# Staggering the two score lanes of a clustered-attention kernel, moving its small pieces, and viewing three VectorE operands interleaved

## The chip, the cores and the metric

The kernel runs on one core of a Trainium2 chip. The metric is the device time of one execution in microseconds; three runs of the kernel before gave 782.86 to 784.72 us, with a median of 783.25 us. Names used for the engines: TensorE (PE in the profile, with PEld for its weight loads), VectorE (DVE), ScalarE (ACT), GpSimd (POOL), and SyncE (SP), which here only issues DMAs.

## The reference

There are 4 batches with 8 heads each, 768 positions and head width 64. Queries and keys are each assigned to one of 16 clusters, and a query attends only to keys of its own cluster. The result is put through a rotation by an angle that depends on the data, a mixing over the positions with two 768 x 768 weights, and a channel layer.

```
q_assign = argmax(q/|q| . centroid/|centroid|)         # per head, 16 clusters; k_assign likewise
mask     = q_assign[:, None] == k_assign[None, :]
scores   = where(mask, q @ k.T / sqrt(64), -1e9)
attn     = softmax(scores)                             # row maximum subtracted, exp, divided by the row sum
x        = (attn @ v) as (batch, 768, 512)
theta    = x @ w_theta;  zr, zi = x*cos(theta), x*sin(theta)
u        = x + w_tok_r @ zr + w_tok_i @ zi
out      = u + relu(u @ w_ch)
```

The weights w_theta, w_tok_r, w_tok_i and w_ch arrive as 64-bit floats; the kernel turns them into 32-bit ones by integer operations, and then into a high and a low part.

## The kernel before, in words

**Two stages.** The attention stage runs from the start to about 440 us, the mixing stage (rotation, mixing, channel layer) from there to the end. The change touches the attention stage alone; the mixing stage uses what it leaves.

**Pairs, lanes, units, bodies.** Two heads are handled together as a pair, so there are 16 pairs. The two heads of a pair are two lanes, `j` = 0 and 1: one has its 64 rows in partitions 0 to 63, the other in 64 to 127, so that a product of one lane and a product of the other can run on TensorE at the same time. A pair has 12 units: two halves of the queries (`a`, 384 columns each) by six blocks of 128 keys (`i`). The main loop at the end of the attention stage handles two units in one body, so a pair takes six bodies, and there are 96 bodies with scores.

**What a unit computes.** `score_products` lists four products for each lane that add up in one PSUM bank, a tile `sc`: high by high, high by low, low by high, and a mask product `mk` by `mq` that also carries the row maximum. `exps` (ScalarE) takes the exponential of the bank into a tile `at`. `add_exps` (GpSimd) adds tiles `at` in threes into `acc`. `weighted` multiplies `at` with the values into the bank `av`, in the following body. Row maxima are found ahead of use: `max_products` computes, ten units ahead (`LEAD`), an approximate score `m` over all 768 keys (two halves of two products for each lane, in a tile of two banks), and `max_of` (VectorE) reduces it. There are two such tiles, one for each lane, so the products of a body can be written only when the reduces of the body before have read theirs. PSUM has eight banks: four in the two `m` tiles, three in the pool that `bank` and the `sc` tiles share, and one for `av`.

**How the products are put in order.** `interleave` takes lists of products and issues them step by step, one of each list. Before, a body issues in this order: `both` (four steps, both lanes of unit u), `scores_beside_max` for j = 0 (four steps, lane 0 of unit u+1 beside the maximum products of lane 1), the weighted products of the two units before, and `scores_beside_max` for j = 1 (four steps). Each group of four steps is followed by its exponentials and its reduce.

**The small pieces.** All else is cut into small pieces and hung at a unit by `at_unit` and `stages`; `pieces` issues what is due at three places of a body. These are, with their tables: the assignment of the clusters for a pair two pairs ahead (`assign`, at `A_UNITS`: load, logits, their transposes and maximum, first maximum, transpose of the result, two rounds of DMA through DRAM, two ScalarE steps for `mq`, one VectorE step for `mk`); the high and low parts of q and k (`HI_UNITS` on ScalarE, `LO_UNITS` on GpSimd); conversion of one block of weights for each pair (`to_f32` and `split_w`, at `W_UNITS`: DMA, ScalarE, four VectorE steps, and then a copy on ScalarE and a subtraction on GpSimd); the row sums (`add_sums` on VectorE at `ADDS`, `sums` at `SUMS`), the division (`normalise` at `NORM`), and `shift_row`, which transposes the maxima and puts them into `mq`.

**What fixes the order.** After each body, `in_order` ties every instruction of an engine to the one before it, SyncE's DMAs too. So within the attention stage every engine works in the order in which the code issues, and an instruction that waits holds up all that its engine has behind it.

Of the kernel before, what the change touches and what calls it, by code (L numbers as in the profile page):

```python
# [2 lines left out]

# [6 lines left out]
F32 = mybir.dt.float32  # L10
# [20 lines left out]
ADDS = (8, 13)  # L31
EARLY = 3
NAT = 6
# [10 lines left out]
def kernel(  # L44
# [79 lines left out]
    def to_f32(src, cols, new):  # L124
# [16 lines left out]
        with behind(weights_after[0]):  # L141
            nc.scalar.activation(out=w, in_=high.bitcast(F32), func=AF.Abs)
        yield
        nc.vector.tensor_scalar(
            out=w, in0=w, scalar1=F64_LEAST, scalar2=F64_MOST, op0=ALU.max, op1=ALU.min)
        yield
        nc.vector.tensor_scalar(
            out=wi, in0=wi, scalar1=5, scalar2=2, op0=ALU.logical_shift_left, op1=ALU.logical_shift_right)
# [182 lines left out]
    def assign(pi):  # L331
# [15 lines left out]
        if "mt" in st.get(pi - 2, {}):  # L347
            mt = st[pi - 2].pop("mt")
            rt = mt[0:NG, P:2 * P]
            nc.tensor.transpose(out=rt, in_=rr, identity=identf)  # L350
# [11 lines left out]
        for n, x in enumerate("qk"):  # L362
# [11 lines left out]
            out=st[pi]["mk"], in0=cl["k"], scalar1=mcl, scalar2=mbi, op0=ALU.not_equal, op1=ALU.mult)  # L374
# [59 lines left out]
    def shift_row(pi, a):  # L434
# [5 lines left out]
        if a == 1 and 0 < pi < NPAIR - 2:  # L440

            s["mt"] = mt
        else:
            shift_out(pi, a, mt)
# [10 lines left out]
    def score_products(u, j, banks=None):  # L455
# [5 lines left out]
        sc = banks[:, j] if banks else ps.tile([P, 512], F32, tag="bank", name=f"sc{u}_{j}")  # L461
        sc = s["sc", j] = sc[:, 0:HS]
# [4 lines left out]
    def exps(u, j):  # L467

        pi, a, i = split_u(u)
        s = st[pi]  # L470
        last_exp[0] = nc.scalar.activation(out=s["at", a, i][:, j], in_=s["sc", j], func=AF.Exp, scale=SCALE)  # L471
# [291 lines left out]
    for pi in range(NPAIR):  # L763
        u = NU * pi
        if pi > 0:
            prepare(pi, g2 if pi == 2 else assign(pi))
            at_unit(u - NU + 7, load_v, pi)
# [15 lines left out]
    u = 0  # L783
    while u <= NUT or todo:
# [8 lines left out]
        if 0 <= u < NUT:  # L793
            both(score_products, u, exps)
            if u == 0:
                for j in range(2):
                    interleave(max_products(ahead - 2, j))
                    max_of(ahead - 2, j)
                for n, x in ((1, "mk"), (0, "mq")):
                    nc.scalar.activation(  # L800
                        out=st[1][x], in_=turn_one_hot(1, n), func=AF.Identity,
                        **(dict(scale=BIG, bias=mbi) if n else {}))
                nc.gpsimd.memset(cl["q"], -100.0)
            add_exps(u)
            if ahead < NUT:
                scores_beside_max(u + 1, ahead, 0)
        pieces(u - 0.5)
        if 0 < u <= NUT:
# [4 lines left out]
            if ahead >= NUT:  # L813
                weighted_out(u - 1)
        pieces(u)
        if 0 <= u < NUT:
            if ahead < NUT:
                scores_beside_max(u + 1, ahead, 1)
            else:

                both(score_products, u + 1, exps, *([m_tile(f"sc{u + 1}")] if u < NUT - 6 else []))
            add_exps(u + 1)
        if 0 < u and ahead < NUT:
            weighted_out(u - 1)
# [274 lines left out]
```

## Time and profile before

| | us |
|---|---|
| median of three runs | 783.25 |
| the profiled execution | 783.16 |
| its span, first to last instruction | 781.4 |
| TensorE busy, whole span | 773.2 (99%) |
| VectorE busy | 567.8 (73%) |
| ScalarE busy | 388.2 (50%) |
| GpSimd busy | 500.6 (64%) |
| one pair in the middle of the attention stage (201.58 to 227.54) | 25.96 |
| of it TensorE / VectorE / ScalarE / GpSimd busy | 25.96 / 24.61 / 17.58 / 25.40 |
| one of the first pairs (96.08 to 122.59) | 26.51 |

How to read it: the ends of matmuls are modelled and matmuls overlap, so that a busy TensorE may still issue more densely; the starts of its instructions tell more than its busy time. Busy time of VectorE and GpSimd contains time in which an instruction has started and stands still. The granted TensorE clock is 1.00 in all stretches.

### The profile page before, as it was taken

Reading aid. Unit: us, or ns where it says so; the run is one execution under the profiler, and the core shown is the slowest. Engines: PE = TensorE matmul, PEld = TensorE weight load, DVE = VectorE, ACT = ScalarE, POOL = GpSimd, SP = SyncE. Lnnn points to the kernel's source line nnn. Section 1 sums busy time; section 2 is a strip of 40 time slices with the busy share of each in tenths; the row PEclk is TensorE's granted clock in tenths of the full one; section 3 lists DMA queues with packets and bytes.
Section 4 is the critical chain, followed back from the end, with each engine's and each line's share of the span. In section 5 each row is a group of like instructions: output and inputs, shape, how many; then the busy total and the mean of one; then the engine's idle time right before and its main releaser. Section 6 shows DMA issues by size and latency. Waiting matters only on the chain.

```text
span 781.4 us, 14422 instructions
## 1 busy us (share of the span) xinstructions
PE 773.2 (99%) x5592; PEld 573.0 (73%) x5592; DVE 567.8 (73%) x689; ACT 388.2 (50%) x780; POOL 500.6 (64%) x289
## 2 busy tenths in 40 slices
PE   9999999999999999999999999999999999999998
PEld 6666565566666666566665588898889988899998
DVE  6789999999999999999989587844344444533322
ACT  3565757576767676767556455432333132503310
POOL 4568888989999999988987667561225112422231
PEclk9999999999999999999999999999999999999999
DMA  4113324432443244425354377124101411120001
GB/s 143 42 60 101 113 63 127 134 100 85 145 134 113 73 144 134 133 69 168 114 203 131 85 219 198 20 58 145 28 15 28 163 27 28 17 92 15 1 21 61
DMA packets 81708, 73.24 MB, mean 94 GB/s; under 512 B 59544, under 2 KB 65512, under 8 KB 81256
## 3 DMA queue, kind: packets, MB, share of 16 engines
q1 hardware_dynamic: 81634, 72.32, 31.2%
q8 instruction: 44, 0.72, 0.4%
q14 instruction: 24, 0.20, 0.1%
q10 hardware_dynamic: 6, 0.00, 0.0%
HBM read 56.89 MB, written 15.31 MB: 92 GB/s over the span
## 4 chain that ended last, share of the span: by engine, by line
PE 92%; DVE 4%; DMA 1%; issue 1%; SPq 1%; ACT 1%; POOL 0%; DVEq 0%
PE y L967 26%; PE sc L408 25%; PE av L543 15%; PE tp L643 7%; PE cy L990 5%; PE m L408 4%; PE cp L990 3%; PE lg L286 1%; PE sm L510 1%; PE y L990 1%; PE lt L299 1%; DVE acc L486 1%; DVE mk L373 1%; PE mt L438 1%; DVE nm L430 1%
## 5 line engine op out<-in xcount | busy, mean ns | idle before, releaser
L471 ACT ACTIVATE at<-sc 128x384 f32<-128x384 f32 x384 | 173.7, 495 | 97.6 <-PE m L408 57.5
L430 DVE TENSOR_REDUCE nm<-m 128x1 f32<-128x768 f32 x192 | 179.8, 946 | 21.0 <-PE m L408 19.9
L482 POOL TENSOR_TENSOR acc<-at,at 128x768 f32<-128x768 f32 x64 | 129.1, 2016 | 34.8 <-ACT at L471 34.8
L408 PE MATMUL m<-hk,hq 64*128 64x384 f32 x384 | 147.7, 385 | 0.8 <-DVE nm L430 0.6
L543 PE MATMUL av<-at,vt 128*64 128x384 f32 x768 | 145.3, 499 | 0.2 <-ACT xt L558 0.2
L918 POOL TENSOR_TENSOR zlc<-ab,zhc 128x512 fp32r<-128x512 f32 x24 | 32.9, 1371 | 162.7 <-ACT zhc L916 162.7
L482 POOL TENSOR_TENSOR acc<-acc,at 128x768 f32<-128x768 f32 x64 | 131.8, 2060 | 7.9 <-ACT at L471 5.7
L408 PE MATMUL m<-mk,mq 64*128 64x384 f32 x384 | 128.1, 334 | 0.0
L408 PE MATMUL sc<-hq,hk 64*128 64x384 f32 x384 | 117.7, 390 | 1.1 <-ACT at L471 0.9
L408 PEld LDWEIGHTS sc<-hq,hk 64*128 64x128 f32 x384 | 56.1, 183 | 61.8 <-issue 24.9
L408 PE MATMUL sc<-lq,hk 64*128 64x384 f32 x384 | 98.3, 335 | 0.0
L408 PE MATMUL sc<-mq,mk 64*128 64x384 f32 x384 | 97.8, 334 | 0.0
L408 PE MATMUL sc<-hq,lk 64*128 64x384 f32 x384 | 97.6, 333 | 0.0
L543 PEld LDWEIGHTS av<-at,vt 128*64 128x64 f32 x768 | 46.5, 136 | 58.6 <-issue 53.7
L408 PEld LDWEIGHTS m<-hk,hq 64*128 64x128 f32 x384 | 70.5, 183 | 3.3 <-DVE nm L430 2.6
L408 PEld LDWEIGHTS m<-mk,mq 64*128 64x128 f32 x384 | 71.1, 185 | 0.2 <-DVE mk L715 0.2
L649 DVE TENSOR_SCALAR kk<-tp 128x512 int32<-128x512 f32 x24 | 16.4, 685 | 73.2 <-PE tp L643 73.2
L486 DVE TENSOR_TENSOR acc<-acc,acc 128x768 f32<-128x768 f32 x30 | 69.0, 2302 | 0.0
L616 ACT CAST xh<-xT 128x512 fp32r<-128x512 f32 x23 | 14.3, 621 | 99.3 <-PE tp L643 99.3
L981 POOL TENSOR_TENSOR ul<-xT,uh 128x384 fp32r<-128x384 f32 (+1 forms) x36 | 33.5, 964 | 35.5 <-ACT uh L980 33.8
L408 PEld LDWEIGHTS sc<-mq,mk 64*128 64x128 f32 x384 | 55.3, 184 | 0.0
L408 PEld LDWEIGHTS sc<-hq,lk 64*128 64x128 f32 x384 | 55.2, 184 | 0.0
(174 smaller groups left out, 1716.3 us busy)
## 6 DMA issues: line engine op xcount, KB each, us to landing
vt<-in_v_dram SPq DMA_DIRECT2D x16, 384.0 KB
rb<-sd SPq DMA_DIRECT2D x32, 192.0 KB
xT_d<-xt SPq DMA_DIRECT2D x16, 384.0 KB
xb<-xT_d SPq DMA_DIRECT2D x96, 64.0 KB
rawq<-in_qT_dram SPq DMA_DIRECT2D x15, 384.0 KB
rawk<-in_kT_dram SPq DMA_DIRECT2D x15, 384.0 KB
w<-in_wrT_dram SPq DMA_DIRECT2D x6, 768.0 KB
xT<-xT_d SPq DMA_DIRECT2D x3, 1536.0 KB
```

Of the source, the lines that this page charges most:

```text
L408: nc.tensor.matmul(out, lhsT=stat[r, cols], rhs=mov[r, over], start=start, stop=stop)
L430: nc.vector.tensor_reduce(out=s["nm", a][:, j, i // 2:i // 2 + 1], in_=s["m", j][:, :, 0:HS], op=ALU.max, axis=AX.XY, negate=True)
L471: last_exp[0] = nc.scalar.activation(out=s["at", a, i][:, j], in_=s["sc", j], func=AF.Exp, scale=SCALE)
L482: last_acc[0] = nc.gpsimd.tensor_tensor(out=s["acc", a, x], in0=prev, in1=at, op=ALU.add)
L486: nc.vector.tensor_tensor(out=s["acc", a, 0], in0=s["acc", a, 0], in1=s["acc", a, 1], op=ALU.add)
L543: nc.tensor.matmul(s["av"][64 * j:64 * j + 64], lhsT=s["vt"][:, i, j, :], rhs=s["at", a, i][:, j], start=(i == 0), stop=(i == NT - 1))
L643: nc.tensor.matmul(tp, lhsT=xx[:, c, :], rhs=w_th[c][k], start=(n == 0), stop=(n == 3 * NCT - 1))
L649: nc.vector.tensor_scalar_mul(kk, tp, INV_2PI)
L918: nc.gpsimd.tensor_tensor(out=zl, in0=tr, in1=zh.bitcast(F32), op=ALU.subtract)
L967: last_mix[0] = nc.tensor.matmul(y_at(b, d, c0, c1), lhsT=zz[:, d * P:(d + 1) * P], rhs=ww[:, c0:c1], start=first and lead, stop=last, ski ...
L981: nc.gpsimd.tensor_tensor(out=ul[:, d, :], in0=x, in1=uh[:, d, :].bitcast(F32), op=ALU.subtract)
L990: nc.tensor.matmul(cp, lhsT=w_c[d][k][:, e * P:(e + 1) * P], rhs=uu[:, d, :], start=(n == 0), stop=(n == 3 * NCT - 1), skip_group_check=True)
```

## The change

1. **Order of the products.** The scores of unit u in lane 0 are begun at the end of the body before (three of four steps, kept in `begun`). A body first issues the pieces due and the weighted products of the two units before, and then one run of twelve steps. In each step a product of one list stands beside a product of another that is one or three steps behind it: the end of lane 0's scores beside the start of lane 1's; the maximum products of lane 0 beside the rest of lane 1's scores; and so on, up to the three first products of the next body's unit in lane 0. Exponentials and reduces follow each list's last step. The two reduces of a body so follow three steps behind each other, with no piece between them.
2. **Small pieces.** The pieces move to other units: `ADDS`, `A_UNITS`, `HI_UNITS`, `LO_UNITS`, `W_UNITS`, and the load of v. The transposes `lt` take a bank of the shared pool and no longer an `m` tile; the transposes `mt` and `rt` no longer share a bank, and the maxima are sent out at once.
3. **Views.** Three VectorE forms work on the same bytes through views in which the second half of the columns is interleaved with the first: the mask `mk`, and the clamp and the shift in `to_f32`.
4. **Buffers.** `at` has 5 buffers in place of 6. For the last units, which have no maximum products, each lane's scores get an `m` tile of their own.

```diff
-ADDS = (8, 13)
+ADDS = (6.5, 14)
-NAT = 6
+NAT = 5
...
+        wt, wit = (x.rearrange("p (a b) -> p b a", a=2) for x in (w, wi))
         nc.vector.tensor_scalar(
-            out=w, in0=w, scalar1=F64_LEAST, scalar2=F64_MOST, op0=ALU.max, op1=ALU.min)
+            out=wt, in0=wt, scalar1=F64_LEAST, scalar2=F64_MOST, op0=ALU.max, op1=ALU.min)
         yield
         nc.vector.tensor_scalar(
-            out=wi, in0=wi, scalar1=5, scalar2=2, op0=ALU.logical_shift_left, op1=ALU.logical_shift_right)
+            out=wit, in0=wit, scalar1=5, scalar2=2, op0=ALU.logical_shift_left, op1=ALU.logical_shift_right)
...
-        lt = (m_tile(f"lt{pi}")[:, 0] if pi > 1 else bank(f"lt{pi}"))[:, 0:HS]
+        lt = bank(f"lt{pi}")[:, 0:HS]
...
-        if "mt" in st.get(pi - 2, {}):
-            mt = st[pi - 2].pop("mt")
-            rt = mt[0:NG, P:2 * P]
-            nc.tensor.transpose(out=rt, in_=rr, identity=identf)
-            shift_out(pi - 2, 1, mt)
-        else:
-            rt = bank(f"rt{pi}")[0:NG, 0:P]
-            nc.tensor.transpose(out=rt, in_=rr, identity=identf)
+        rt = bank(f"rt{pi}")[0:NG, 0:P]
+        nc.tensor.transpose(out=rt, in_=rr, identity=identf)
...
         nc.vector.tensor_scalar(
-            out=st[pi]["mk"], in0=cl["k"], scalar1=mcl, scalar2=mbi, op0=ALU.not_equal, op1=ALU.mult)
+            out=st[pi]["mk"].rearrange("p (a b) -> p b a", a=2), in0=cl["k"].rearrange("p (a b) -> p b a", a=2),
+            scalar1=mcl, scalar2=mbi, op0=ALU.not_equal, op1=ALU.mult)
...
-    A_UNITS = (-9, -4, -2, -1, 2, 2, 3, 6, 7, 7.9)
-    HI_UNITS = dict(q=-0.5, k=1.5)
-    LO_UNITS = dict(q=2, k=4)
-
-    W_UNITS = (8, 11.5, 14, 15, 16, 18, 19.5)
+    A_UNITS = (-6, -1.5, 0, 1, 6, 6, 7, 9.5, 11.5, 11)
+    HI_UNITS = {'q': 2.5, 'k': 5.0}
+    LO_UNITS = {'q': 5.5, 'k': 7}
+
+    W_UNITS = (7, 12.5, 14, 15, 15, 17, 19.5)
...
+    def products(u, j):
+        return score_products(u, j) if u < NUT else []
+
+    def both_lanes(p0, p1):
+
+        for x in zip_longest(p0, p1):
+            interleave(*([y] for y in x if y))
+
+    u, begun = 0, products(0, 0)
+    interleave(begun[:3])
...
         pieces(u - 0.5)
         if 0 < u <= NUT:
             weighted(u - 2)
             ...
             weighted(u - 1)
-            if ahead >= NUT:
-                weighted_out(u - 1)
+            weighted_out(u - 1)
         pieces(u)
         if 0 <= u < NUT:
+            a0, a1 = begun[3:], products(u, 1)
+            m = [max_products(ahead, j) for j in range(2)] if ahead < NUT else None
+            both_lanes(a0, a1[:1])
+            exps(u, 0)
+            if m:
+                both_lanes(m[0][:3], a1[1:])
+                exps(u, 1)
+                add_exps(u)
+                both_lanes(m[0][3:], m[1][:1])
+                max_of(ahead, 0)
+                b0 = products(u + 1, 0)
+                both_lanes(b0[:3], m[1][1:])
+                max_of(ahead, 1)
+                b1 = products(u + 1, 1)
             else:
...
+            both_lanes(b0[3:], b1[:1])
+            exps(u + 1, 0)
...
+            begun = products(u + 2, 0)
+            both_lanes(begun[:3], b1[1:])
+            exps(u + 1, 1)
             add_exps(u + 1)
         pieces(u + 1)
```

In the positions of a pair (units 0 to 11 of a pair's twelve, as they come round), VectorE's pieces move like this: `mk` from 7.9 to 11.5, the two maxima on the logits from 10 to 0, the first maximum from 11 to 1, the sums from 8 and 1 to 6.5 and 2, and the four steps of the weights from 2, 3, 4, 6 to 2, 3, 3, 5.

More of the change, by code (lines that the diff above doesn't have):

```diff
@@ L2 @@
 from contextlib import ExitStack, nullcontext
+from itertools import zip_longest
 import concourse.bass as bass
@@ L439, in shift_row @@
             out=mt[0:NT, 0:P], in_=s["nm", a].rearrange("p j t -> p (j t)"), identity=identf)
[L440 to L444, printed above, removed]
+        shift_out(pi, a, mt)
     def shift_out(pi, a, mt):
@@ L460, in score_products @@
             s["at", a, i] = p3.tile([P, 2, HS], F32, tag="at", name=f"at{u}", bufs=NAT)
-        sc = banks[:, j] if banks else ps.tile([P, 512], F32, tag="bank", name=f"sc{u}_{j}")
-        sc = s["sc", j] = sc[:, 0:HS]
+        sc = banks[:, j] if banks is not None else ps.tile([P, 512], F32, tag="bank", name=f"sc{u}_{j}")
+        sc = s["sc", u, j] = sc[:, 0:HS]
         k, q = slice(i * P, (i + 1) * P), slice(a * HS, (a + 1) * HS)
@@ L470, in exps @@
         s = st[pi]
-        last_exp[0] = nc.scalar.activation(out=s["at", a, i][:, j], in_=s["sc", j], func=AF.Exp, scale=SCALE)
+        last_exp[0] = nc.scalar.activation(out=s["at", a, i][:, j], in_=s["sc", u, j], func=AF.Exp, scale=SCALE)
     def add_exps(u):
@@ L766 @@
             prepare(pi, g2 if pi == 2 else assign(pi))
-            at_unit(u - NU + 7, load_v, pi)
+            at_unit(u - NU + 7.5, load_v, pi)
         for a in range(2):
@@ L780 @@
     stages([NUT - 10 + k for k in FIRST], first_rotation())
-    u = 0
+    def products(u, j):
[5 more added lines that the diff above has]
+    interleave(begun[:3])
     while u <= NUT or todo:
@@ L791, in pieces @@
                     fn(*a)
[L793 to L806, printed above, removed]
         pieces(u - 0.5)
@@ L812 @@
             weighted(u - 1)
-            if ahead >= NUT:
-                weighted_out(u - 1)
+            weighted_out(u - 1)
         pieces(u)
         if 0 <= u < NUT:
-            if ahead < NUT:
-                scores_beside_max(u + 1, ahead, 1)
-            else:
-                both(score_products, u + 1, exps, *([m_tile(f"sc{u + 1}")] if u < NUT - 6 else []))
+            if u == 0:
+                both(max_products, ahead - 2, max_of)
+            a0, a1 = begun[3:], products(u, 1)
[12 more added lines that the diff above has]
+                b1 = products(u + 1, 1)
+            else:
+                b0, b1 = (score_products(u + 1, j, m_tile(f"sc{u + 1}_{j}") if u < NUT - 6 else None) for j in range(2))
+                both_lanes(b0[:3], a1[1:])
+                exps(u, 1)
+                add_exps(u)
+            both_lanes(b0[3:], b1[:1])
+            exps(u + 1, 0)
+            if u == 0:
+                for n, x in ((1, "mk"), (0, "mq")):
+                    nc.scalar.activation(
+                        out=st[1][x], in_=turn_one_hot(1, n), func=AF.Identity,
+                        **(dict(scale=BIG, bias=mbi) if n else {}))
+                nc.gpsimd.memset(cl["q"], -100.0)
+            begun = products(u + 2, 0)
+            both_lanes(begun[:3], b1[1:])
+            exps(u + 1, 1)
             add_exps(u + 1)
-        if 0 < u and ahead < NUT:
-            weighted_out(u - 1)
         pieces(u + 1)
```

## The prediction

> **What bounds the kernel now.** I read the chain of waits first, then the busy time of one pair of heads, then the order of time on each engine inside a pair.
>
> ```profile
> PE 92%; DVE 4%; DMA 1%; issue 1%; SPq 1%; ACT 1%; POOL 0%; DVEq 0%
> core 0: us, PE busy (x) PEld busy (x) DVE busy (x) ACT busy (x) POOL busy (x), PEclk, DMA share, GB/s
> 96.08:122.59 26.51, 26.31 (x216) 16.01 (x214) 26.25 (x26) 17.05 (x38) 23.92 (x13) 1.00 0.35 104
> 201.58:227.54 25.96, 25.96 (x216) 15.85 (x214) 24.61 (x26) 17.58 (x38) 25.40 (x13) 1.00 0.36 117
> 441.79:781.50 339.71, 335.83 (x2022) 303.26 (x2020) 163.21 (x267) 110.21 (x191) 120.08 (x95) 1.00 0.26 68
> ```
>
> The chain lies on TensorE for 92% of the span, at a full clock. The change leaves the last 339.7 us (rotation, mixing) as they are, so it works on 441.8 us. There a pair takes 25.96 us, in the first pairs 26.51. Three engines stand close together: TensorE fills the pair, GpSimd is busy for 25.40 of it, VectorE for 24.61; in the first pairs VectorE is busy for 26.25 of 26.51 and sets the pace. Whatever makes TensorE faster meets the other two almost at once.
>
> One body on TensorE, in order of time (the second row of a pair of lanes is left out):
>
> ```profile
> 211.32 0.44 PE L408 MATMUL sc<-hq,hk 64*128 64x384 f32 x1
> ...
> 212.13 0.33 PE L408 MATMUL sc<-hq,hk 64*128 64x384 f32 x2
> ...
> 212.65 0.34 PE L408 MATMUL sc<-mq,mk 64*128 64x384 f32 x2
> 212.87 0.44 PE L408 MATMUL sc<-hq,hk 64*128 64x384 f32 x1
> ...
> 213.15 0.34 PE L408 MATMUL sc<-lq,hk 64*128 64x384 f32 x1
> ...
> 213.77 1.51 PE L543 MATMUL av<-at,vt 128*64 128x384 f32 x8
> 215.21 0.27 PE L438 MATMUL mt<-identf,nm 128*6 128x128 f32 x1
> 215.32 0.27 PE L350 MATMUL mt<-identf,rr 128*24 128x128 f32 x1
> ```
>
> Steps that follow on each other start 0.173 us apart (212.13 to 212.65 is three). The first step of a run takes 0.28 (212.87 to 213.15), and 0.05 more lie before it: it begins 0.22 behind its forerunner, since a bank has to come free. From the last of the four steps (213.15 + 2 x 0.173 = 213.50) to the weighted products it is 0.27. So the twelve steps take 2.45 us (211.32 to 213.77) with two starts, and the weighted products 1.44 (213.77 to 215.21).
>
> **Part 1, the run of twelve steps.** The same products are issued; only their order changes. One start in place of two: 0.28 + 10 x 0.173 + 0.27 = 2.28, or 0.17 less; I count 0.16 for each body. Maximum products exist in the bodies of units 0 to 180, 91 of them: **-14.6 us**. The bank that a step needs is now freed by an exponential three to eight steps back, and no longer by the last one; so the wait at 212.87 goes too. The weighted products come right behind the last scores:
>
> ```profile
> L471 ACT ACTIVATE at<-sc 128x384 f32<-128x384 f32 x384 | 173.7, 495 | 97.6 <-PE m L408 57.5
> 219.40 0.85 PE L510 MATMUL sm<-acc,ecol 128*32 128x384 f32 x8
> ```
>
> Lane 1 of their second unit starts 3 x 0.36 = 1.1 after the run (1.44 for four such), its exponential is ready 0.5 and some 0.2 of handing over (my estimate) after it. I cost that at nothing; ScalarE's spare time covers it (17.58 busy of 25.96), and without it each 0.1 would cost 9 us.
>
> **Part 2, the small pieces on TensorE.** `mt` and `rt` went together, 0.11 apart; as pieces of two bodies I put them 0.1 a pair dearer. `lg` now comes directly behind the run and takes the bank of the exponential three steps before its end: 0.7 - 3 x 0.173 = 0.2 of waiting. Together +0.35 at most, for 14 pairs: **+4.9 us** (least +1.4).
>
> **Part 3, the order on VectorE.** This is the part I trust least.
>
> ```profile
> 202.72 2.60 DVE L486 TENSOR_TENSOR acc<-acc,acc 128x768 f32<-128x768 f32 x1
> ...
> 209.40 1.39 DVE L311 TENSOR_TENSOR eq<-eq,wc 128x384 bf16<-128x384 bf16 x1
> 210.83 0.55 DVE L313 TENSOR_REDUCE rr<-eq 128x24 f32<-128x384 bf16 x1
> ...
> 215.47 0.94 DVE L430 TENSOR_REDUCE nm<-m 128x1 f32<-128x768 f32 x1
> 216.33 1.33 DVE L144 TENSOR_SCALAR w<-w 128x768 f32<-128x768 f32 x1
> ...
> 220.56 1.71 DVE L150 SCALAR_TENSOR_TENSOR w<-w,w 128x768 int32<-128x768 int32 x1
> ```
> ```profile
> 202.34 2.17 POOL L482 TENSOR_TENSOR acc<-at,at 128x768 f32<-128x768 f32 x1
> 204.59 2.42 POOL L482 TENSOR_TENSOR acc<-acc,at 128x768 f32<-128x768 f32 x1
> ...
> 208.76 1.82 POOL L482 TENSOR_TENSOR acc<-at,at 128x768 f32<-128x768 f32 x1
> ```
> ```profile
> L486 DVE TENSOR_TENSOR acc<-acc,acc x30: 950/2309/2605, 42.3 to 420.6; 128x768 f32<-128x768 f32 x30
> L311 DVE TENSOR_TENSOR eq<-eq,wc x16: 347/1392/1670, 9.1 to 365.2; 128x384 bf16<-128x384 bf16 x16
> ```
>
> (The last two rows give the least, the median and the longest ns.) Two things are to be seen. VectorE and GpSimd exclude each other in these forms: the sum at 202.72 stands until GpSimd's instruction ends at 204.51, works 0.81 to 205.32, and GpSimd's next, begun at 204.59, takes 2.42 in place of 1.82. And before, a reduce stands between nearly any two heavy pieces. After, VectorE has, between the reduces of one body and the next, the product on the one-hots, its maximum, a sum and a weight step; and then two weight steps in a row. The two reduces of a body start 0.87 apart (215.47 and 216.33), and both must end before the same steps of the next body.
>
> From the start of body 0's run: logit maxima until 1.2, second reduce until 2.94. Body 2's run starts at 2.28 + 1.44 + 0.2 = 3.92, body 4's 2.28 + 1.44 + 0.8 later (0.8 for the row sums, the `sm` row above), at 8.4; its fifth step, at 9.2, writes lane 1's tile, so the reduces of body 2 must start by 9.2 - 0.87 - 0.95 = 7.4: room for 4.4. With the durations of these rows (2.31 for the sum) the four pieces take 1.39 + 0.55 + 2.31 + 1.33 = 5.6, 5.3 when the 0.08 by which rows overlap are taken off; with the least, 0.35 + 0.55 + 0.95 + 0.95 = 2.8. For the next two room is 1.9, and the need 1.7 to 3.0. So TensorE stands between 0 and 0.9 + 1.1 = 2.0 us in each pair. It depends on who asks first: VectorE is free for the one-hots at 2.94, GpSimd's addition of unit 1 becomes ready at 2.28 + 0.7 = 2.98. If VectorE goes first, they take 0.9, the sum waits out an addition until 2.94 + 0.35 + 1.82 = 5.1 and ends at 5.95, the weight step at 6.9, in time. I take **0.3 a pair, +4.2 us**: near the lower end, because with part 4 the two engines meet less often.
>
> **Part 4, the views.**
>
> ```profile
> L373 DVE TENSOR_SCALAR mk<-clk,mcl,mbi 128x768 fp32r<-128x768 f32 x14 | 21.5, 1536 | 0.0
> L430 DVE TENSOR_REDUCE nm<-m 128x1 f32<-128x768 f32 x192 | 179.8, 946 | 21.0 <-PE m L408 19.9 <-PE sc L408 0.2
> L147 DVE TENSOR_SCALAR spare<-spare x2: 362/363/364, 410.8 to 416.2; 128x384 int32<-128x384 int32 x2
> 421.54 2.20 DVE L144 TENSOR_SCALAR w<-w 128x768 f32<-128x768 f32 x1
> ```
>
> The plain form left alone takes 0.36 us for 384 elements, less than half of the 0.95 of a reduce over 768: it is the faster kind, and one that stands behind GpSimd (1.54 on the mean for 768). No row shows an interleaved one. Either it stays as it is (1.54, 1.33: a gain of nothing), or it falls to one element at a time without GpSimd's company: about the 0.95 of a reduce over 768. I take the second: the two halves are then no longer two separate runs. That frees some 0.6 for the mask and 0.4 for each weight step, 1.3 us of VectorE in a pair, and 3 x 0.35 = 1.05 of GpSimd (2.17 against 1.82 beside a mask). In the steady pairs this is cover for part 1, not time on the path: GpSimd's 25.40 would not fit into 25.1, its 24.35 does. On the path it counts in the first five pairs, half of their excess of 0.55 (**-1.4**), and at the end of the stage, where the clamp's 2.20 and a shift as long stand in VectorE's way: 0 to -2.4, I take **-1.0**.
>
> [...]
>
> **Part 5, at nothing.** Five `at` buffers: an addition has some two bodies before its tile is written again, and GpSimd is not that late. If it were, ScalarE would stop, then TensorE; bound 0 to +5. SyncE's order: the load of the next raw k waits for GpSimd's low part of q, and the cluster maps stand behind it; ScalarE takes those 2.5 units later, before 3.
>
> ```profile
> 219.35 0.77 SPq L364 DMA_DIRECT2D clq<-rd  x2
> 223.17 0.93 ACT L369 ACTIVATE mq<-clq,ncl 128x768 fp32r<-128x768 f32 x1
> ```
>
> 3.8 us lay between issue and use, without a wait. Half a unit less is 1.1 us less; a late map stops ScalarE, but the 1.44 of weighted products follow on TensorE. I take 0, bound +0.5 a pair.
>
> **Sum.** -14.6 + 4.9 + 4.2 - 1.4 - 1.0 = -7.9. The profiled execution took 783.16 us, 1.8 around its span of 781.4; the median, 783.25, is the same to 0.1. Forecast **775 us**, its own range 766 to 781.
>
> **Rivals.**
> *The heavy pieces of VectorE stop TensorE* (slower). GpSimd asks first: the one-hots stand until 4.8, the sum behind a multiplication until 7.0, the weight step ends near 8.8, 1.4 late: 14 x 1.4 = 19.6. 783.2 - 14.6 + 4.9 + 19.6 - 2.4 = **791**; 799 with all of the 2.0. It decides from (14.6 - 4.9 + 2.4) / 14 = 0.86 a pair. For it speaks the long median of the sums (2309 against 950), against it that VectorE is first by my times.
> *The views change nothing and GpSimd holds the pace* (no change): 25.40 busy and the 0.56 of waits that a pair shows now, 25.96 again, **783**. For it speaks that GpSimd is this full already; against it that a part of its 25.40 is standing behind VectorE.
> *Everything fits* (faster): no stop, `lg` not waiting, the first pairs and the end relieved whole: -14.6 + 1.4 - 2.7 - 2.4 = -18: **765**.
>
> **Numbers.** The forecast 0.5, the stop 0.27, no change 0.12, everything fits 0.11. 0.3% is 2.3 us, about what a measurement of this kernel tells from no change. Faster by more 0.6, within 0.13, slower 0.27. The range 763 to 791 takes in the fastest case and half of the slow one.
>
> **What would show it.** Twelve steps 0.173 apart with one start, and 2.3 from there to the weighted products (part 1). Waits of TensorE's weight loads on the reduces (`m` on `nm`) in the bodies of units 4 and 6: none or 0.3 a pair, or 1.4 and more (part 3). The three forms at 0.95 with little spread, or at 1.2 to 2.1 as now (part 4). A pair at 25.4; GpSimd's busy time near 24.3. The mixing stage unchanged at 339.7. I am wrong if a pair is no shorter than 25.96, or if the gain lies outside the pairs.

## The result, and the profile after

| | before | after |
|---|---|---|
| median, us | 783.44 | 834.18 |
| the profiled execution, us | 783.16 | 833.96 |
| its span, us | 781.4 | 832.2 |
| last weighted product, us from the start | 441.4 | 485.8 |
| from there to the end of the span, us | 340.0 | 346.4 |

The kernel is slower: the ratio is 1.065, 95% interval 1.063 to 1.068. One of the four executions of the kernel after took 2544.98 us and is left out of the 834.18 (with it the median is 835.31, from which some of the expectations below count). The forecast was 775 us, faster. Of the 51 us that the span grew, 44.4 lie in the attention stage and 6.4 in the mixing stage, which the change does not touch.

The chain of waits of the kernel after, by engine and by line, and busy time in three stretches (two pairs and the mixing stage):

```profile
PE 47%; DVE 23%; DMA 12%; issue 6%; SPq 4%; POOL 4%; ACT 3%; DVEq 0%; ACTq 0%; POOLq 0%
PE y L979 18%; DMA sq<-sd 9%; DVE nm L427 7%; PE tp L636 5%; PE av L536 5%; PE cy L1002 5%; PE sc L405 4%; PE m L405 4%; PE cp L1002 3%; DVE mk L369 3%; POOL lq L391 3%; DVE w L146 2%; DVE acc L479 2%; SPq L360 2%; POOL acc L475 2%
```
```profile
112.57:140.83 28.26, 26.88 (x215) 16.51 (x214) 22.55 (x25) 18.17 (x37) 23.93 (x12) 1.00 0.31 98
258.57:288.33 29.76, 27.49 (x215) 16.55 (x214) 23.57 (x25) 18.39 (x37) 24.62 (x12) 0.96 0.31 102
486.21:832.20 345.99, 338.97 (x2022) 305.54 (x2020) 166.00 (x267) 109.92 (x190) 118.57 (x95) 0.99 0.25 66
```

The chain lay on TensorE for 92% of the span, and now for 47%; 9% of it is one load, `sq`, the row sums on their way to VectorE's reciprocal. A pair takes 28.3 and 29.8 us in place of 25.96, and no engine is full in it: TensorE is busy for 26.9 and 27.5 us, VectorE for 22.6 and 23.6, GpSimd for 23.9 and 24.6. So the engines wait for each other. Waits by engine and releaser (us in total, times, longest), first of all engines, then of SyncE's queue:

```profile
DVE sq L521 <- DMA sq<-sd: 65.5, 15, 6.2
PEld m L405 <- DVE nm L427: 24.8, 58, 2.7
PE sc L405 <- DVE eq L308: 16.1, 12, 2.3
PE m L405 <- DVE nm L427: 10.8, 22, 2.4
...
SPq L279 <- POOL lq L391: 33.0, 13, 2.9
```

Before, VectorE waited 3.0 us in all for `sq`. What happened to that load is seen in order of time, on SyncE's queue, VectorE and TensorE, in one pair of the kernel after (start, duration, and in brackets idle time with what ended it):

```profile
328.38 0.34 SPq L279 DMA_DIRECT2D rawq<-in_qT_dram  x1
331.72 0.33 SPq L279 DMA_DIRECT2D rawk<-in_kT_dram  x1
332.48 0.79 SPq L360 DMA_DIRECT2D clq<-rd  x2
334.29 0.37 SPq L137 DMA_DIRECT2D w<-in_wrT_dram  x1
334.71 0.43 SPq L380 DMA_DIRECT2D vt<-in_v_dram  x1
335.19 0.42 SPq L519 DMA_DIRECT2D sq<-sd  x1
...
340.81 0.23 DVE L521 RECIPROCAL sq<-sq 128x12 f32<-128x12 f32 x1 [5.39 <-DMA sq<-sd]
340.96 1.75 DVE L427 TENSOR_REDUCE nm<-m 128x1 f32<-128x768 f32 x2
342.63 1.53 DVE L369 TENSOR_SCALAR mk<-clk,mcl,mbi 128x768 fp32r<-128x768 f32 x1
343.98 0.53 DVE L306 TENSOR_REDUCE mxl<-lt 128x24 f32<-128x384 f32 x1
```

Raw k waits 3.3 us on the queue for GpSimd's low part of q (328.38 to 331.72). Behind it stand the cluster maps, 768 KB of weights, 384 KB of v, and only then `sq`, which is in use 5.6 us after its issue. VectorE stands at the reciprocal for 5.4 us with all else behind it: two reduces that had long been ready, the mask and the comparison of the logits. In all, TensorE waits for the bank in which the logits' transposes `lt` lie (`sc` on `eq`) and for the reduces (`m` on `nm`). Which of these stops hang on the load is for the runs to tell.

One body in which nothing stands shows the run of steps as the change means it (TensorE, in order of time):

```profile
318.15 0.44 PE L405 MATMUL sc<-hq,hk 64*128 64x384 f32 x1
318.43 0.33 PE L405 MATMUL m<-hk,hq 64*128 64x384 f32 x1
...
320.46 1.52 PE L536 MATMUL av<-at,vt 128*64 128x384 f32 x8
```

From its first step to the weighted products it is 2.31 us; before it was 2.45.

### The profile page after: what moved, and what is told of

It is laid out like the page before. It is cut to its first block, busy times and chain, and to the rows that moved or that the text cites. A ratio compares the mean times of both kernels' runs of the same rounds, so it can differ in the third digit from the quotient of the medians.

```text
span 832.2 us, 14405 instructions
## 1 busy us (share of the span) xinstructions
PE 792.6 (95%) x5592; PEld 586.0 (70%) x5592; DVE 547.3 (66%) x689; ACT 404.7 (49%) x780; POOL 497.1 (60%) x289
## 4 chain that ended last, share of the span: by engine, by line
PE 47%; DVE 23%; DMA 12%; issue 6%; SPq 4%; POOL 4%; ACT 3%; DVEq 0%; ACTq 0%; POOLq 0%
PE y L979 18%; DMA sq<-sd 9%; DVE nm L427 7%; PE tp L636 5%; PE av L536 5%; PE cy L1002 5%; PE sc L405 4%; PE m L405 4%; PE cp L1002 3%; DVE mk L369 3%; POOL lq L391 3%; DVE w L146 2%; DVE acc L479 2%; SPq L360 2%; POOL acc L475 2%
## 5 line engine op out<-in xcount | busy, mean ns | idle before, releaser
L464 ACT ACTIVATE at<-sc 128x384 f32<-128x384 f32 x384 | 184.6, 490 | 109.2 <-PE sc L405 103.1
L427 DVE TENSOR_REDUCE nm<-m 128x1 f32<-128x768 f32 x192 | 173.7, 946 | 27.0 <-PE m L405 26.9
L405 PE MATMUL sc<-hq,hk 64*128 64x384 f32 x384 | 124.6, 382 | 17.9 <-DVE eq L308 16.1
L405 PE MATMUL sc<-mq,mk 64*128 64x384 f32 x384 | 138.2, 362 | 0.0
L405 PE MATMUL m<-hk,hq 64*128 64x384 f32 x384 | 125.7, 354 | 11.2 <-DVE nm L427 10.8
L405 PE MATMUL m<-mk,mq 64*128 64x384 f32 x384 | 119.7, 338 | 0.0
L405 PE MATMUL sc<-lq,hk 64*128 64x384 f32 x384 | 110.5, 344 | 0.0
L405 PE MATMUL sc<-hq,lk 64*128 64x384 f32 x384 | 106.9, 335 | 0.0
L405 PEld LDWEIGHTS sc<-mq,mk 64*128 64x128 f32 x384 | 71.1, 185 | 29.7 <-issue 24.3
L405 PEld LDWEIGHTS m<-hk,hq 64*128 64x128 f32 x384 | 71.0, 186 | 25.8 <-DVE nm L427 24.8
L405 PEld LDWEIGHTS sc<-hq,hk 64*128 64x128 f32 x384 | 64.4, 184 | 27.6 <-issue 15.2
L405 PEld LDWEIGHTS sc<-hq,lk 64*128 64x128 f32 x384 | 64.4, 185 | 0.0
L405 PEld LDWEIGHTS sc<-lq,hk 64*128 64x128 f32 x384 | 61.8, 185 | 0.0
```

Source lines behind the costliest of these rows:

```text
L405: nc.tensor.matmul(out, lhsT=stat[r, cols], rhs=mov[r, over], start=start, stop=stop)
L427: nc.vector.tensor_reduce(out=s["nm", a][:, j, i // 2:i // 2 + 1], in_=s["m", j][:, :, 0:HS], op=ALU.max, axis=AX.XY, negate=True)
```

## The experiments

The theories, by the letters of the expectations. Q: the order on SyncE's queue makes the row sums late, and all else follows. V: the interleaved views still exclude GpSimd and are slower. H, later C: VectorE's heavy pieces meet in one gap between reduces. C2: VectorE is too full, wherever its pieces stand. L and K: the staggered run loses by itself, because banks come free late behind ScalarE's pieces. Each time is a median with the ratio to the kernel before and its 95% interval.

### The views

After, with the three forms on plain views:
```diff
-        wt, wit = (x.rearrange("p (a b) -> p b a", a=2) for x in (w, wi))
-            out=wt, in0=wt, scalar1=F64_LEAST, scalar2=F64_MOST, op0=ALU.max, op1=ALU.min)
+            out=w, in0=w, scalar1=F64_LEAST, scalar2=F64_MOST, op0=ALU.max, op1=ALU.min)
...
```


> The changed kernel with the three VectorE forms on plain views again; all else as changed. Theory Q (SyncE's order: the load of raw k waits for GpSimd, and the DMAs of the row sums and of the cluster maps stand behind it): the 65.5 us of VectorE's wait before the reciprocal stay, and the time moves little, 825 to 836 us. Theory V (the interleaved forms still exclude GpSimd and take one element at a time, so that they cost more than before): the clamp falls from 2.6 to about 1.4 us, the shift and the mask by some tenths, 12 to 20 us come back, 815 to 823. Theory H (the heavy pieces of VectorE in a row stop TensorE, the first rival of the prediction): about 1.3 us a pair less in that row, 815 to 825 as well, so this run tells Q from the other two.

Before, with the interleaved views and nothing else:
```diff
+        wt, wit = (x.rearrange("p (a b) -> p b a", a=2) for x in (w, wi))
-            out=w, in0=w, scalar1=F64_LEAST, scalar2=F64_MOST, op0=ALU.max, op1=ALU.min)
+            out=wt, in0=wt, scalar1=F64_LEAST, scalar2=F64_MOST, op0=ALU.max, op1=ALU.min)
...
```


> The kernel before with part 3 of the change alone: the three VectorE forms on interleaved views. The prediction's fourth part: each form takes about 0.95 us and lets GpSimd run; 1 to 3 us less, 780 to 782. [...] V: each form waits for GpSimd as before and then works 0.8 in place of 0.4 us; VectorE's 24.6 us a pair become 25.8 and GpSimd's 25.4 become 26.3, so the pair grows to 26.3 or more: 787 to 797.

Measured: 824.3 us for the first (1.052, 1.050 to 1.054), 9.9 under after, just outside the ranges of V and of Q and inside that of H; 794.3 for the second (1.013, 1.011 to 1.015), 10.9 over before, inside that of V alone. So the second run decides for V, and the first agrees in size. In the first, VectorE's wait for `sq` stayed, at 70.1 us. Forms of the second kernel (times in ns: least, median, longest), VectorE and GpSimd around one mask, and a stop of TensorE:

```profile
L148 DVE TENSOR_SCALAR spare<-spare x2: 513/519/525, 420.5 to 425.9; 128x384 int32<-128x384 int32 x2
L374 DVE TENSOR_SCALAR mk<-clk,mcl,mbi x14: 1149/2270/2731, 52.1 to 392.9; 128x768 fp32r<-128x768 f32 x14
...
230.79 2.68 DVE L374 TENSOR_SCALAR mk<-clk,mcl,mbi 128x768 fp32r<-128x768 f32 x1
...
230.78 1.84 POOL L484 TENSOR_TENSOR acc<-at,at 128x768 f32<-128x768 f32 x1
232.69 3.22 POOL L484 TENSOR_TENSOR acc<-acc,at 128x768 f32<-128x768 f32 x1
...
263.22 0.55 PE L300 MATMUL lt<-identf,lgs 128*128 128x128 f32 x3 [1.59 <-DVE nm L432]
```
The mask in the kernel before:
```profile
L373 DVE TENSOR_SCALAR mk<-clk,mcl,mbi x14: 1220/1224/2292, 51.7 to 383.4; 128x768 fp32r<-128x768 f32 x14
```

Alone, 384 elements take 519 ns in place of 363. For the mask's 768, where GpSimd rests beside it, it is 1.10 us in the kernel after (from 373.00) and 0.67 in the run with plain views (from 365.67). So the views are slower, near the 0.95 of a reduce over 768 that the prediction took for them. But GpSimd is still shut out. The mask that starts at 230.79 stands until GpSimd's addition ends at 232.62 and needs 0.85 more; GpSimd's next, started at 232.69, stands behind the mask and the sum that follows it on VectorE (233.21 to 234.24), and takes 3.22. The mask's median goes from 1224 to 2270. Where mask and sum meet GpSimd one after the other (2.63 us from 257.32, 2.56 from 259.74), the reduce comes late, and TensorE stops for 1.59 us before `lt`, which in the kernel before lies in an `m` tile. The cost is uneven: three of the first pairs are even shorter than before (25.95 against 26.50), for a reason that is not shown, and three later ones take 28.1 to 29.5.

### The loop alone

Before, with the new order of products; pieces, banks (`lt` in an `m` tile), buffers and views as before:
```diff
+    u, begun = 0, products(0, 0)
+            both_lanes(a0, a1[:1])
...
+            begun = products(u + 2, 0)
+            both_lanes(begun[:3], b1[1:])
```


> The kernel before with part 1 of the change alone: the staggered run of twelve steps; tables, banks of the small pieces, five or six buffers and views as before. The prediction's first term: 14.6 us less, 765 to 772 us. Rival: the begun scores hold one of three banks across the pieces, and the old tables put two small pieces into one body, so that TensorE waits for a bank there, 0.5 us or more in a pair: 775 to 790 us.

Measured: 807.5 (1.031, 1.029 to 1.032), worse than either theory gave; its pairs from the sixth on take 27.5 us. Waits by releaser:

```profile
PEld m L409 <- DVE nm L431: 11.8, 23, 2.6
PEld lt L300 <- DVE nm L431: 11.7, 11, 1.3
PEld sc L409 <- ACT at L472: 10.6, 39, 0.9
```

Stops come from VectorE's reduces (`m`, and `lt`, which lies in an `m` tile) and from the exponentials (`sc` on `at`). To tell them apart, the four VectorE steps of the weights were left out, in the kernel before as a control and in this one:

```diff
-        yield
-        nc.vector.tensor_scalar(
-            out=w, in0=w, scalar1=F64_LEAST, scalar2=F64_MOST, op0=ALU.max, op1=ALU.min)
...
+        for _ in range(4):
+            yield
```


> A control: the kernel before, with the four VectorE steps of the weights' conversion left out in the attention stage (the weights then have wrong values; loads, ScalarE's and GpSimd's parts stay). TensorE bounds it, so only the first pairs and the end of the stage can gain: 774 to 782. If it gained more than 14, VectorE would bound the steady pairs too.

> The staggered loop alone (807.5 us) with the same four VectorE steps left out (weights wrong). Theory C (the loop loses because reduces and heavy pieces on VectorE stand together, so that the tiles of the maximum products come free late): with some 6 us less on VectorE in each pair the stops go, and the twelve steps show what they are worth: 762 to 770, and 10 to 15 below the control. Rival K (the banks of the scores, which ScalarE's exponentials free too late, stop the staggered run): VectorE has no part in it, 795 to 803, and 18 to 25 above the control.

Measured: control 779.6 (0.996, 0.994 to 0.997), loop alone 790.5 (1.009, 1.007 to 1.010). So without these steps the loop gains 17.0 and the kernel before 3.5: 13.5 of the loop's 24 us hang on these steps of VectorE, for which the new order leaves less room. The other 10.9 are something else; neither C nor K had the whole. In the loop alone without the steps:

```profile
PEld sc L399 <- ACT at L462: 10.9, 42, 0.4
PE m L399 <- DVE eq L297: 3.6, 14, 0.3
```

I read both as matters of place. In the tables of before, ScalarE's pieces stand between the weighted products and the run, ahead of the exponential of the run's first step; and `lt` lies in the tile that the run needs at its second step. Moving ScalarE's pieces and `lt` ahead of the weighted products, and spreading VectorE's pieces, was tried next:

```diff
-    A_UNITS = (-9, -4, -2, -1, 2, 2, 3, 6, 7, 7.9)
+    A_UNITS = (-9, -4, -2.5, -1, 2, 2, 3, 5.5, 7.5, 7.9)
-SUMS = (4, 6, 8, 9, 10)
+SUMS = (3.5, 6, 8, 9, 10)
```


> The staggered loop alone (807.5 us) with ScalarE's pieces and the logits' transposes put ahead of the weighted products in place of behind them (A_UNITS -2 to -2.5, 6 to 5.5, 7 to 7.5; SUMS 4 to 3.5). In the loop alone TensorE's steps stood 33 us in all by their starts: 6.7 on exponentials, 5.5 on VectorE's comparison of the logits, 12.3 on reduces. Theory K: ScalarE's pieces stood between the weighted products and the run, ahead of the exponential of the run's first step; with 1.44 us of weighted products to cover them, the waits on exponentials halve and those on the comparison go: 793 to 798. Rival C2: VectorE is full in any order, and the reduces take up what is freed: 803 to 810.

```diff
-    A_UNITS = (-9, -4, -2.5, -1, 2, 2, 3, 5.5, 7.5, 7.9)
-    W_UNITS = (8, 11.5, 14, 15, 16, 18, 19.5)
+    A_UNITS = (-9, -4, -2.5, -1, 2, 2, 3, 5.5, 7.5, 8.9)
+    W_UNITS = (8, 11.5, 15, 16, 17, 18, 19.5)
```


> The kernel of the first run of this call, and VectorE's heavy pieces spread over the six gaps between pairs of reduces (mask from 7.9 to 8.9, the weights' four steps from 2, 3, 4, 6 to 3, 4, 5, 6), so that no gap has two of the longest. Theory C: the reduces wait because two heavy pieces fall into one gap; another 5 to 9 us less: 785 to 792. Rival C2 (24.6 us of work on VectorE do not fit into pairs of six gaps, wherever they stand): no more than 3 us less.

Measured: 818.7 (1.044, 1.043 to 1.046) and 817.5 (1.043, 1.042 to 1.045), both a miss. In the first:

```profile
PE lt L300 <- DVE nm L431: 25.5, 11, 2.5
```

The earlier `lt` now asks for its `m` tile before the reduce of the body before has read it. So this place for `lt` does not go with the staggered loop at all, and the two runs say nothing on the spreading.

### The order of loads

After, with the raw loads later:
```diff
-    A_UNITS = (-6, -1.5, 0, 1, 6, 6, 7, 9.5, 11.5, 11)
+    A_UNITS = (-3.5, -1.5, 0, 1, 6, 6, 7, 9.5, 11.5, 11)
```


> The changed kernel with one number different: the load of the raw q and k at unit 8.5 of a pair in place of 6, behind the other DMAs. Q: SyncE's waits for the low part of q (33.0 us) go, VectorE's wait before the reciprocal falls from 65.5 us to under 15, ScalarE's wait for the cluster map (8.6 us) goes, and 25 to 40 us come back: 795 to 810 us. H and V: the pair is limited elsewhere, the reciprocal comes earlier and nothing follows: 828 to 836.

Measured: 821.9 (1.051, 1.047 to 1.055), 12.3 us less, about half of the least that Q wanted; VectorE's wait for `sq` fell to 30.2 us and no further, as the weights still stood ahead of it. With those moved too, and plain views:

```diff
-    W_UNITS = (7, 12.5, 14, 15, 15, 17, 19.5)
+    W_UNITS = (8, 12.5, 14, 15, 15, 17, 19.5)
```


> The kernel after with three edits: the three VectorE forms on plain views, the raw loads at unit 8.5 (A_UNITS[0] = -3.5), and the load of the weights at unit 8 in place of 7, so that the small load of the row sums no longer stands behind 768 KB. Theory Q (the row sums come late for VectorE, which then clumps): with the raw loads alone the waits of VectorE's reciprocal on that load fell from 65.5 to 30.2 us; with the weights behind it they should fall under 10, and the time to 795 to 803 (835.3 - 11.0 for the views - 13.4 for the raw loads, and 8 to 16 more). Rival L (the staggered loop itself costs 24 us, and the tables cost nothing beyond what was undone): 806 to 812, no lower than the loop alone (807.5).

> The kernel of the first run of this call (plain views, small loads first) with the four VectorE steps left out (weights wrong). Theory C: 765 to 775. Rival K: 790 or more; what then stops it besides the banks is the logits' transposes, which hold a bank of the scores until VectorE has compared them.

Measured: 835.9 (1.067, 1.065 to 1.069) and, with the steps left out, 819.1 (1.047, 1.043 to 1.051). `sq` came earlier, but the raw loads now stood behind the weights:

```profile
PE lg L287 <- DMA rawq<-in_qT_dram: 24.5, 12, 3.3
DVE sq L519 <- DMA sq<-sd: 13.6, 9, 3.6
```

The two runs judge nothing but this new mistake. With the raw loads directly behind `sq`, and the weights behind both, first with plain views, then with the views of the change:

```diff
-    A_UNITS = (-6, -1.5, 0, 1, 6, 6, 7, 9.5, 11.5, 11)
-    W_UNITS = (7, 12.5, 14, 15, 15, 17, 19.5)
+    A_UNITS = (-4, -1.5, 0, 1, 6, 6, 7, 9.5, 11.5, 11)
+    W_UNITS = (9.5, 12.5, 14, 15, 15, 17, 19.5)
```


> The kernel after with plain views, the raw loads at unit 8 and the load of the weights behind them at 9.5 (they were at 6 and 7; with 8.5 and 8 the raw loads stood behind the weights and TensorE waited 28.9 us for them in front of the logits). Theory Q: neither the row sums nor the raw loads are late; the 28.9 us go, and of the 14.7 of the comparisons and 9.0 of the reduces that the plain views had left, at least half: 803 to 809. Rival: other small loads (cluster maps, rb) take the place, 815 to 825.

> The kernel after with its interleaved views and only the order of loads changed (raw loads at 8, weights at 9.5; 800.8 with plain views). Theory V: the views cost what they cost alone, 11 us: 810 to 814. Rival (they cost only where VectorE is already late for the row sums): 801 to 805; more than 815 if they clump the heavier with less idle time on VectorE.

Measured: 800.8 (1.022, 1.020 to 1.024) and 810.9 (1.035, 1.032 to 1.037). The first is a little better than Q gave, the second as V gave. With only the places of these loads moved, the kernel after gains 23.3 us (834.2 to 810.9); with plain views in both, 23.4 (824.3 to 800.8). The views cost 10.0 here, so the two costs add up. This also answers L: tables and order of loads cost far more than was undone until then. The second run, which differs from the kernel after by the loads alone, shows what hangs on them:

```profile
DVE sq L521 <- DMA sq<-sd: 5.1, 4, 2.6
PEld m L405 <- DVE nm L427: 21.6, 53, 2.7
```

VectorE's wait for `sq` falls from 65.5 to 5.1 us, and the stops of `sc` on `eq` (16.1) are gone. The stops of `m` on `nm` stay, 21.6 of 24.8; with plain views as well they fall too:

```profile
PEld m L403 <- DVE nm L425: 8.2, 16, 2.6
PEld lg L287 <- DMA rawk<-in_kT_dram: 8.0, 10, 1.4
```

So they hang on the views more than on the loads (15.6 with plain views and the loads unchanged). The last row is new: the kernel after, which loads raw k earlier, has no such wait.

### Is the run sound?

On that kernel (plain views, loads mended), VectorE's heavy pieces were spread, and then the last blocks of weights too:

```diff
-ADDS = (6.5, 14)
-    W_UNITS = (9.5, 12.5, 14, 15, 15, 17, 19.5)
+ADDS = (9, 14)
+    W_UNITS = (9.5, 12.5, 15, 16, 17, 19, 20.5)
```


> The kernel of the third run of this call, and VectorE's heavy pieces spread (the weights' four steps from 2, 3, 3, 5 to 3, 4, 5, 7, the first half's sum from 6.5 to 9). In the kernel after, the first maximum, a sum and a weight step fell into one gap. Theory C: 6 to 12 us below that run, 793 to 800. Rival C2: within 3 us of it.

```diff
-    W_LAST = ((169, 172, 176, 176, 177, 177, 178.5), (169.5, 172.5, 178, 178, 179, 179, 180.5))
+    W_LAST = (
+        (176.5, 178.5, 180, 181, 182, 183, 184.5), (164, 166, 167, 167, 168, 168, 169.5),
+        (165, 170.5, 174, 174, 178, 178, 179.5))
```


> The kernel with plain views, the weights behind the raw loads and VectorE's heavy pieces spread (797.4 us), and the last three blocks of weights converted elsewhere: their VectorE steps, which stood together at units 176 to 179 and 183 to 187, at 167, 168, 174, 178 and 180 to 183. In that kernel TensorE stood 3.2 us in one place at 419 us, on a reduce, with weight steps in front of it, and its first channel layer stood for 2.3 us on weights that came late. Theory C (gaps with too much VectorE work): the last pair falls from 30.2 to 26 or less and the time to 789 to 794. Rival: the place of the last blocks has nothing to do with it, 796 to 799.

Measured: 797.4 (1.018, 1.016 to 1.020), 3.4 less, where C gave 6 to 12 and C2 at most 3; and 797.2 (1.017, 1.014 to 1.020), no gain: the last pair fell from 30.2 to 26.3, the one before rose from 24.2 to 25.3, and other pairs and the mixing stage took up the rest. Then the logits:

```diff
-    A_UNITS = (-4, -1.5, 0, 1, 6, 6, 7, 9.5, 11.5, 11)
-    W_UNITS = (9.5, 12.5, 15, 16, 17, 19, 20.5)
+    A_UNITS = (-4, -0.5, 1, 3, 6, 6, 7, 9.5, 11.5, 11)
+    W_UNITS = (9.5, 12.5, 16, 17, 19, 20, 21.5)
```


> The first run of this call, and the logits and their transposes one unit later (-1.5 to -0.5, 0 to 1; the first maximum 1 to 3, the weights' four steps to 4, 5, 7, 8), so that the raw loads have landed and the transposes stand ahead of weighted products. Before it, five of the six bodies of a pair were 3.95 to 4.53 apart, the body with the logits 5.0 to 6.0, of which 3.75 and 0.75 would be the work. If the staggered run is worth what was forecast once nothing stands in it (theory: the loop is sound, its surroundings cost it), a pair takes 25.1 to 25.4 and the time is 778 to 785. If the run has a loss of its own (rival K), pairs stay at 25.9 or more: 788 or more.

Measured: 795.9 (1.016, 1.015 to 1.018). By the numbers set for it this spoke for a loss of the run itself, but the logits had not moved, as -1.5 and -0.5 are one place in the code. Moved to 0, and then with six buffers:

```diff
-    A_UNITS = (-4, -0.5, 1, 3, 6, 6, 7, 9.5, 11.5, 11)
+    A_UNITS = (-4, 0, 1, 3, 6, 6, 7, 9.5, 11.5, 11)
```


> The kernel with the logits' transposes one unit later (795.9 us), and the logits themselves from -0.5 to 0, which is the first place behind the next body's weighted products (-0.5 and -1.5 are the same place, at the end of a body's run, so the logits had not moved). In that kernel five bodies of a pair were 3.93 to 4.51 apart and the one with the logits 4.7 to 6.8, waiting for raw k by up to 1.3 us. Theory (the run is sound): with 1.4 us more the load has landed, a pair takes 25.2 to 25.5 in place of the 25.5 to 28.0 there, and the time is 780 to 786, no slower than before by more than 3 us. Rival K (a loss of its own): pairs of 25.9 or more, 790 or more.

```diff
-NAT = 5
+NAT = 6
```


> The same with six buffers of exponentials in place of five. If the fifth buffer was enough, as forecast, the same to 1 us; if GpSimd's late additions held ScalarE and so TensorE, 2 to 5 us less.

Measured: 790.0 (1.010, 1.008 to 1.012) and 785.4 (1.003, 1.002 to 1.004). The first missed the 780 to 786 set for it and lies at the edge of K's; its pairs are on both sides, 25.3 to 25.7 up to 183 us, and 26.0 to 26.8 after, but for one. The first pairs settle the question, since a loss of the run itself would be in every pair. Busy time in the kernel with six buffers (two pairs, the mixing stage), then one pair of the kernel before:

```profile
82.31:107.60 25.29, 25.25 (x215) 16.09 (x214) 23.75 (x25) 18.16 (x39) 23.71 (x13) 1.00 0.34 110
289.42:315.74 26.32, 25.77 (x216) 16.38 (x215) 24.68 (x25) 18.49 (x38) 25.11 (x13) 1.00 0.36 110
443.85:783.06 339.21, 335.99 (x2024) 303.33 (x2020) 161.91 (x267) 110.04 (x191) 118.82 (x95) 1.00 0.26 68
```
```profile
82.32:108.81 26.49, 26.29 (x217) 15.98 (x215) 26.21 (x25) 17.13 (x38) 23.90 (x13) 1.00 0.35 105
```

Two pairs side by side, 25.29 against 26.49. VectorE was full in the latter (26.21 busy), so only a part of this is the run's; but 25.29 is also below the 25.96 of a later pair before, which TensorE fills. The run has no loss of its own. A later pair with six buffers takes 26.3. There, on VectorE and on TensorE:

```profile
286.89 2.25 DVE L368 TENSOR_SCALAR mk<-clk,mcl,mbi 128x768 fp32r<-128x768 f32 x1
289.07 1.80 DVE L425 TENSOR_REDUCE nm<-m 128x1 f32<-128x768 f32 x2
...
291.37 0.56 DVE L307 TENSOR_TENSOR eq<-lt,mxl 128x384 bf16<-128x384 f32 x1
...
292.08 0.41 PE L403 MATMUL sc<-hq,hk 64*128 64x384 f32 x1 [0.51 <-DVE eq L307]
```

A mask of 2.25 us makes the reduces late, these the comparison, and the run stops for the bank of `lt`. So mask and sum changed places, and the last blocks were spread again:

```diff
-ADDS = (9, 14)
-    A_UNITS = (-4, 0, 1, 3, 6, 6, 7, 9.5, 11.5, 11)
+ADDS = (11, 14)
+    A_UNITS = (-4, 0, 1, 3, 6, 6, 7, 9.5, 10, 10)
...
```


> The kernel with six buffers (785.4 us), and three pieces of VectorE moved: the mask from 11.5 to 10, the first half's sum from 9 to 11, and the last blocks' steps, two to four of which stood in one gap at units 167, 168, 178 and 180, to one or two a gap. In that kernel the pairs took 25.22 to 25.58 up to 159 us and 26.0 to 26.5 after, where a mask of 2.25 us in the gap ahead of a pair's first body made the logits' comparison late (body 0 took 4.6 to 4.9 in place of 3.94), and the last two pairs stood 4.7 us on reduces. Theory C (it is the contents of a gap that count): those pairs return to 25.3 to 25.7 and the time is 775 to 781, faster than before. Rival (whatever gap the mask and the sum stand in, GpSimd's longer subtractions of the later weights make it late): 783 to 787.

Measured: 787.4 (1.005, 1.003 to 1.006), at the rival's end. The stops on the comparison went, but the code makes the mask behind `mq`'s second ScalarE step, and that now stood ahead of a run's first exponential:

```profile
PEld sc L403 <- ACT at L462: 8.8, 28, 1.3
```

Pairs are 25.5 to 26.3 in all, the early ones longer than without this edit. So that the late mask is what lengthens the later pairs is read from the waits and not shown. No version beat the kernel before; the nearest is 0.3% behind it.

### The mixing stage

Between the runs with five and six buffers the attention stage is the same (last weighted product at 443.0 and 443.8 us) and the mixing stage goes from 344.3 to 339.2 us. ScalarE's conversion of the weights kept in DRAM (the last two times are the first and the last start in us), with five buffers:

```profile
L891 ACT CAST wr_hi<-kept x3: 832/834/841, 467.8 to 476.2; 128x768 fp32r<-128x768 f32 x3
```
The same line with six:
```profile
L891 ACT CAST wr_hi<-kept x3: 828/834/836, 459.8 to 470.3; 128x768 fp32r<-128x768 f32 x3
```

With five it begins 24.8 us behind the last weighted product, with six 16.0; the kernel before, with six, has 15.5 by the same line. The kernel after has the late start too (25.3), and in its channel layer TensorE waits:
```profile
PE cp L1002 <- ACT uh L992: 2.6, 1, 2.6
...
PE cy L1002 <- ACT uh L992: 1.0, 1, 1.0
```
That the number of buffers does it is shown by this pair of runs, and the others agree: with five the stage takes 343.1 to 347.3 us, with six 339.2 to 341.8. One run stands apart: with five buffers and the four VectorE steps left out, the conversion starts as late (25.4) and the stage takes 339.5, as with six. So the late start alone is not the cost. By what way the buffers do it (the memory that the mixing stage takes over, or the order that its planner makes of it) is open.

## Why the prediction was wrong, point by point

**The run of twelve steps (-14.6).** Mechanism and size were right where nothing stands in the run: 2.31 us to the weighted products against the 2.28 forecast; bodies without small pieces are 3.74 us long in the first pairs of the kernel with six buffers, by the starts of their weighted products, 3.89 before, 0.15 against 0.16. That the waits for banks go is right in the main for the new tables (weight loads of `sc` on exponentials 16.6 us before, 5.3 after, 3.1 with six buffers), though less so for the loop in general (10.6 in the loop alone).

**Small pieces on TensorE (+4.9).** The pair of 25.29 us less six bodies of 3.74 leaves 2.85 for the pieces; before, 25.96 less six of 3.89 leaves 2.62. That is +0.23 a pair, inside the +0.1 to +0.35 given; both rests contain what waits a pair has. Missed was that `lt`'s bank is freed by VectorE (16.1 us of waits in after). The waits of `lg` for raw k, which moving the logits took off, are no miss of the prediction: the later raw loads of the mended runs brought them in.

**VectorE's heavy pieces (+4.2).** The size is not settled. Spreading them gained 3.4 once loads and views were mended, near the 4.2, but that is what one new place took off and not what the old one cost: in the loop alone, with the old tables, the four steps of the weights cost 13.5 more than before, and the later pairs with six buffers still show a stop behind the mask. The rival of 791 had the direction right, but its path is at most a part of what was measured. The sum held only while VectorE came to its pieces on time.

**The views (-2.4).** Wrong in sign: +9.9 to +10.9. Half of the step holds: they get slower, to about the pace of a reduce (519 ns in place of 363 for 384 elements; 1.10 us for a mask of 768 where GpSimd rests, 0.95 for a reduce over 768). The other half, "without GpSimd's company", is what failed: the mask that starts at 230.79 stands until GpSimd's addition ends at 232.62. The prediction did not bound this case: a form that is slower and still exclusive.

**Part 5, at nothing.** This is the step that decided. "SyncE's order: the load of the next raw k waits for GpSimd's low part of q, and the cluster maps stand behind it" was costed 0, with a bound of 0.5 a pair, by following the maps alone to their user. The load of the row sums stands behind the same wait and behind 1152 KB more, and its user, the reciprocal, has all of VectorE's reduces behind it. Another order of these loads alone took 23.3 to 23.4 us off, 1.7 for each of 14 pairs, and with it the waits on `sq` and on the comparison. The five buffers, 0 with a bound of 5, cost 4.7 (785.4 against 790.0), but in the mixing stage, which was forecast as unchanged.

**The account.** From 834.2: plain views -9.9 (824.3), loads -23.4 (800.8), heavy pieces -3.4 (797.4), last blocks and the next shift -1.6 (795.9), logits -5.8 (790.0), buffers -4.7 (785.4). The order is that of the runs, and the logits' 5.8 belong in part to the loads. The first five pairs gain 4.1 us (127.5 in place of 131.6 between their first weighted products); the pairs after them and the end of the stage take back 5.3. So parts 1 and 2, which were to bring -9.7 together, stand at +2.0 with all this undone. Of the 12 us between, 6.8 are the seven pairs from 184.3 us on, 26.26 on the mean in place of 25.29, whose cause is open as said; for the rest no run was made.

## What to carry to other kernels

Where engines work in a fixed order, follow each moved transfer to every transfer behind it on its queue, and each of those to its user and to what that user's engine has behind it; a bound on the transfer that is named bounds nothing. A tighter order on the engine that sets the pace takes slack from all others: measure it together with the places of the pieces around it, since a pair with the same run of products took 25.29 us with one set of places and 27.5 with another, where the kernel before takes 25.96. Before a stage is called unchanged, ask what it inherits: a buffer fewer in one stage went with 5 us in the next.

## What the runs showed of the hardware

A VectorE form with one source over two halves interleaved, the shift, took 519 ns for 384 elements in place of 363, and the interleaved mask still stood until GpSimd's addition ended (230.79 to 232.62, the rows above). And a stop of TensorE can cost more than itself: behind two of them the granted clock was 0.50. In the kernel with heavy pieces spread, one reduce held TensorE for 3.2 us near the end of the stage; in the kernel after, a comparison held it for 1.8 us at 255.41. The granted clock (the third number from the end) in the stretch of each stop and in one behind it:

```profile
418.70:422.30 3.60, 0.45 (x4) 0.19 (x2) 3.57 (x5) 0.87 (x2) 1.61 (x1) 1.00 0.96 297
422.95:426.36 3.41, 3.41 (x20) 2.72 (x20) 3.38 (x6) 1.20 (x3) 0.00 (x0) 0.50 0.19 67
```
```profile
255.41:257.24 1.83, 0.00 (x1) 0.03 (x2) 1.80 (x4) 0.49 (x1) 0.00 (x0) 1.00 0.66 200
257.48:260.89 3.41, 3.41 (x15) 1.42 (x13) 3.38 (x5) 1.29 (x2) 1.65 (x1) 0.50 0.00 0
```

For 3.4 us the clock is at half; behind the first stop, steps are 0.32 us apart in place of 0.17. Not every such stop was followed by that: behind one of 2.04 us at 225.67 in the kernel after the clock was 1.00 (227.71 to 231.10). So stops of 3.2 and 1.8 us came ahead of half a clock and one of 2.04 did not; what decides it is not shown.
